# Loads of q and k by tile pairs, another pairing of heads, a shorter distance table, and a new order of all units

## The chip, the cores and the metric

The kernel runs on one core of a Trainium2 chip. The metric is the device time of one execution in microseconds, the median of several runs. Five engines of the core work side by side, each on its own queue of instructions in order: TensorE (PE in the profile, with its weight loads as PEld), VectorE (DVE), ScalarE (ACT), GpSimd (POOL), and SyncE (SP), which here only issues DMA transfers. They wait for one another by semaphores.

## What is computed

A causal attention with a local window and a few global keys, followed by a feed-forward layer that takes the maximum of three products:

```python
# q, k, v: (4 batches, 8 heads, 768 positions, 64), fp32;  n_global = 8, n_local = 96
scores = q @ k^T / sqrt(64)
rel = pos[:, None] - pos[None, :]
is_global = pos[None, :] < 8
is_local = (rel >= 0) & (rel < 96)
dist = where(is_global & ~is_local, 96, abs(rel))
scores = scores - slope[h] * dist          # slope[h] = 2 ** -(h + 1)
a = softmax(where(is_global | is_local, scores, -1e9))
x = (a @ v) as (3072 tokens, 512)
h = max(x @ w1, x @ w2, x @ w3)            # 512 -> 768
out = h @ w_out                            # 768 -> 512, fp32
```

The matrix products run in bf16 with fp32 sums.

## The kernel before

**Tiles.** The 3072 tokens are 24 tiles of 128, six per batch. A query tile needs its own key tile, the tile before it and the eight global keys. The global keys need no step of their own: the first eight rows of the key tile before are overwritten by the global ones (put_kg for k, put_vg for v) once that tile has served as its own.

**Units.** The work is cut into units, and a string, SCHEDULE, names them one after another; the loop at the end of the kernel (lines 479 and 480) calls them in that order, and every engine gets its instructions in the order of the calls. Nothing reorders them. A unit is a letter with numbers; the last number often chooses the engine (0 ACT, 1 DVE, 2 POOL).

- `l`, `c`, `x` (load_part, cast_part, u_x): for tiles 0 to 11, load q or k of a group of tiles from memory (SP), cast to bf16, transpose on TensorE into PSUM and copy back ("evacuate") into qkT, which holds head dimension by position. `L`, `C`, `X` (load, cast, u_X) do this tile by tile for tiles 12 to 23; with how = 4 a DMA transpose takes the place of TensorE and the evacuation. `v` and `C..1` load and cast v.
- `K` and `B` (u_K, u_B): from the table rbase of distances make, per head, a mask exp(-slope x distance) on ACT, or a bias -slope x distance. rbase is the distance where a key is allowed and 60000 where not.
- `S` (u_S): the scores of four heads of a tile, 64-row products on TensorE, and their exp on ACT into P. With how = 1 two further products with the identity add the bias; otherwise `M` (u_M) multiplies P by the mask on DVE.
- `A` (u_A): P times v with a column of ones, on TensorE; on DVE the reciprocal of the sums and the product into xb. `T` (u_XT) transposes xb into xT, on TensorE or (how = 4) by DMA.
- `F` (u_F1): for a chunk of two or four tiles, one of six column blocks f and one of three weights j: four products into a PSUM tile of the pool psH, which has three buffers. j = 0 is copied out by ACT, j = 1 and 2 are merged by DVE's maximum into ht. `O` (u_F2) and, for the last chunk, `E` (u_E): six products per tile with w_out, copy, and the output DMA.
- `w`, `W`, `o`, `Q`: loads and bf16 casts of the weights. `D`: products with zeros, which nobody reads. `G`, `V`: put_kg and put_vg.

**Ahead of the units** (lines 443 to 474) stand the first two loads, the table rbase, the identity for the transposes, and fills.

**Layout of q and k in tiles 0 to 11.** GROUPS cuts them into groups of 2, 2, 2, 4 and 2 tiles. A partition holds sz consecutive positions of every head of the part, so that a row of 64 x sz floats is contiguous in memory: 512 bytes for two tiles, 1 KB for four. A transpose takes a pair of neighbouring heads (2j, 2j + 1) of one of the sz positions; the evacuation puts the positions back in order. A score product of one head uses 64 of 128 rows, and two heads that lie in the two halves run side by side.

Of the kernel before, what the change touches and what calls it, by code (L numbers as in the profile page):

```python
# [12 lines left out]
FP32 = mybir.dt.float32  # L13
# [24 lines left out]
    O0.1.1 S9.1.0 S9.0.0 V7.1 M8.0 T6.0 x4.0.3 F1.2.2 M8.1 O0.2.1 M9.0 M9.1 C8.1.0 F2.5.0 F2.0.0
    G9.2 S10.0.0 S10.1.0 G10.2 F1.3.2 C9.1.2 F2.0.1 F2.0.2 A8.0 X12.0 F2.2.0 C13.0.3 V8.2 A9.1 X13.4
    T8.4 T9.4 F2.4.0 F2.5.1 C14.0.1 X14.4 v15 F2.4.1 S11.0.0 S11.1.0 O1.1.0 M11.0 M10.1 M10.0 F2.2.1  # L40
    S12.0.0 S12.1.0 F2.2.2 M11.1 F2.5.2 V9.2 C10.1.2 A10.0 V10.1 C11.1.2 L15 O1.0.0 F2.1.0 F2.4.2
    C13.1.2 A11.0 T10.0 F2.1.1 F2.3.0 S13.1.0 G12.0 S13.0.0 L18 T11.1 M12.1 F2.3.1 F2.3.2 M12.0
    G13.2 C15.1.2 L16 v14 C14.1.2 F3.5.0 F3.4.0 F3.4.1 F2.1.2 C12.1.0 M13.1 S14.0.0 M14.0 C15.0.0
    X15.4 S14.1.0 F3.5.1 M13.0 F3.1.0 A12.0 M14.1 F3.4.2 F3.2.0 F3.0.0 A13.0 V13.0 F3.1.1 C16.0.0
    G14.0 F3.2.1 F3.2.2 L19 F3.3.0 C18.0.0 X16.0 L17 F3.1.2 S15.1.0 S15.0.0 C19.0.1 T12.4 G15.0
    F3.3.1 F3.0.1 F3.0.2 X18.4 T13.4 C17.0.0 A14.1 F3.3.2 V14.1 F3.5.2 M15.0 X19.4 S16.0.0 L20 T14.4
    S16.1.0 M16.1 v18 C18.1.2 v17 v16 O2.0.0 X17.4 O3.2.0 S18.0.0 v19 S18.1.0 G16.0 O3.3.0 M15.1
    A15.0 V15.0 O3.1.0 C20.0.1 M18.1 X20.4 T15.0 M18.0 O3.0.0 F4.3.0 A18.0 M16.0 F4.2.0 F4.0.0
    S19.1.0 M19.1 C16.1.0 S19.0.0 L21 F4.0.1 F4.3.1 L22 A16.1 C19.1.0 L23 T16.4 F4.3.2 F4.2.1 G18.0
    V16.0 M19.0 F4.2.2 T18.4 S17.0.0 S17.1.0 F4.1.0 F4.5.0 F4.5.1 G19.2 M17.1 F4.1.1 A19.1 F4.1.2  # L50
    M17.0 F4.4.0 C17.1.2 F4.4.1 C21.0.3 F4.4.2 S20.0.0 S20.1.0 C22.0.1 F4.0.2 T19.4 F4.5.2 v20 X21.4
    A17.0 T17.4 O4.0.0 C23.0.0 X22.4 v21 O4.3.1 v22 V19.1 G20.0 O4.2.1 v23 O4.1.1 S21.0.0 S21.1.0
    F5.2.0 F5.1.0 M20.0 M21.0 M20.1 F5.1.1 C20.1.2 F5.5.0 F5.1.2 A20.1 M21.1 G21.2 F5.0.0 F5.2.1
    S22.0.0 V20.0 S22.1.0 G22.2 F5.5.1 F5.5.2 F5.0.1 F5.4.0 M22.0 C21.1.0 X23.4 S23.1.0 M23.1
    S23.0.0 F5.4.1 F5.4.2 A21.1 T21.4 V21.2 C22.1.2 M23.0 T20.4 O2.1.0 M22.1 F5.3.0 F5.3.1 C23.1.0
    F5.0.2 A22.0 T22.4 F5.2.2 F5.3.2 V22.2 A23.0 T23.4 O5.3.1 O5.0.1 O5.2.1 O5.1.1 F6.3.0 F6.1.0
    F6.1.1 F6.0.0 F6.4.0 F6.0.1 F6.4.1 F6.4.2 F6.5.0 F6.5.1 F6.1.2 F6.2.0 F6.2.1 F6.0.2 F6.2.2
    F6.3.1 F6.3.2 F6.5.2 E D2.8 D0.3
# [4 lines left out]
def kernel(  # L63
# [29 lines left out]
    GROUPS = [[0, 2], [2, 2], [4, 2], [6, 4], [10, 2]]  # L93
# [27 lines left out]
    identf = persist.tile([128, 128], FP32, name="identf")  # L121
# [24 lines left out]
    def part(n, s):  # L146

        T0, sz = GROUPS[n]
        jn = {2: 4, 4: 2, 6: 1}[sz]
        a, x = divmod(s, 4 // jn)  # L150
        return divmod(T0, NT) + (sz, a, x * jn, jn)

    def load_part(n, s):

        bb, t0, sz, a, j0, jn = part(n, s)
        r = raw_pool.tile([128, 2 * DM], FP32, name="rawp", tag="raw")
        r = r[:, 0:sz * jn * 128].rearrange("i (h x) -> i h x", h=2 * jn)
        raw["p", n, s] = r
        src = (q, k)[a][bb, 2 * j0:2 * (j0 + jn), t0 * 128:(t0 + sz) * 128, :]
        nc.sync.dma_start(out=r, in_=src.rearrange("h (i e) d -> i h (e d)", e=sz))  # L160
# [19 lines left out]
    def cast_part(n, s, how):  # L180
        bb, t0, sz, a, j0, jn = part(n, s)
        qk = cast_pool.tile([128, 2 * DM], BF16, name="qkp", tag="qkb")
        qk = qk[:, 0:sz * jn * 128].rearrange("i (e h d) -> i e h d", e=sz, d=D)
        qb["p", n, s] = qk
        copies[how](qk, raw["p", n, s].rearrange("i h (e d) -> i e h d", e=sz))  # L185

    def cast(T, what, how):
        b, t = divmod(T, NT)
        if what == 1:
            va[T] = va_first[b % 2] if t == 0 else va_ring[T % NVA]  # L190
            copies[how](heads(va[T])[:, :, 0:D], rawv[T])  # L191
# [3 lines left out]
        flat = raw[T].rearrange("p a h d -> p a (h d)")  # L195
        if how == 3:
            nc.vector.tensor_copy(qk[:, 0], flat[:, 0])
            nc.gpsimd.tensor_copy(qk[:, 1], flat[:, 1])
        else:
            copies[how](qk, flat)  # L200
# [27 lines left out]
    def u_x(n, s, how):  # L228
        bb, t0, sz, a, j0, jn = part(n, s)
        dst = batch_T(bb)[:, a, j0:j0 + jn, t0 * 128:(t0 + sz) * 128].rearrange("c j (i e) -> c j i e", e=sz)  # L230
        if how >= 4 and jn > 1:
            m = jn // 2
            halves = [(0, m, psT, "tp", nc.scalar.copy), (m, jn, psH, "h", nc.vector.tensor_copy)]
        else:
            pool, tag = (psH, "h") if how in (2, 3) else (psT, "tp")
            halves = [(0, jn, pool, tag, copies[how % 2])]
        tps = [pool.tile([128, sz, hi - lo, 128], BF16, name="tpp", tag=tag) for lo, hi, pool, tag, copy in halves]
        for (lo, hi, pool, tag, copy), tp in zip(halves, tps):
            for e in range(sz):
                for j in range(lo, hi):  # L240
# [273 lines left out]
```

## Time and profile before

| | |
|---|---|
| median of 3 runs (lowest to highest) | 178.89 us (178.78 to 180.11) |
| the profiled execution's own time | 179.17 us |
| its span | 177.4 us |
| TensorE clock granted, mean | 0.99 |
| PE busy | 170.6 us, 96% |
| DVE busy | 126.5 us, 71% |
| ACT busy | 109.7 us, 62% |
| POOL busy | 19.9 us, 11% |
| DMA packets, bytes | 85,730, 36.04 MB |

The page and the answers of the trace belong to one execution. The span begins with the first instruction that the profile shows and ends with the last; some 1.8 us of the execution lie outside it. Busy times are shares of the span, and an engine may be busy with work that nobody waits for. A busy share above 1 for DMA means that packets overlap on the 16 DMA engines. In the chain that ended last each step is followed back to what released it. A group of instructions is told by its line, engine, operation and tiles (out<-in).

### The profile page before, as it was taken

What the parts mean: (1) busy time and instruction counts of PE and PEld (TensorE: products, weight loads), DVE (VectorE), ACT (ScalarE), POOL (GpSimd) and SP (SyncE); (2) the same over time, 40 slices, a digit from 0 to 9 for tenths busy, and PEclk for the clock granted to TensorE, in tenths of its full rate; (3) what the DMA queues carried; (4) which work ended last, traced back from release to release, by engine and by line L of the source; (5) the groups of instructions that cost most, each with busy time, mean ns of one, the idle gap of its engine ahead of it and who ended that gap; (6) DMA issues with size and microseconds to landing.
All of it is one profiled execution on the core that took longest, in us unless ns stands there. A gap on an engine that the chain in (4) does not pass through costs nothing.

```text
span 177.4 us, 3967 instructions
## 1 busy us (share of the span) xinstructions
PE 170.6 (96%) x1550; PEld 95.7 (54%) x1550; DVE 126.5 (71%) x248; ACT 109.7 (62%) x166; POOL 19.9 (11%) x46
## 2 busy tenths in 40 slices
PE   7586899999999999999999999999999999999997
PEld 2344645458766786855554555455454555444444
DVE  4678969889697999769677557597667597435710
ACT  4979998758797967677595667615456630132022
POOL 4022300100130171010100011101000020000000
PEclk9879999999999999999999999999999999999999
DMA  5999999999999999899999999997796015600006
GB/s 146 291 234 271 344 343 381 321 356 325 289 211 221 241 301 147 214 242 204 213 175 186 208 245 248 231 164 148 176 300 91 0 33 134 218 32 0 4 21 215
DMA packets 85730, 36.04 MB, mean 203 GB/s; under 512 B 68304, under 2 KB 80464, under 8 KB 85712
## 3 DMA queue, kind: packets, MB, share of 16 engines
q1 hardware_dynamic: 85568, 35.73, 86.4%
q8 instruction: 12, 0.20, 0.5%
q10 hardware_dynamic: 144, 0.07, 0.1%
q14 instruction: 6, 0.05, 0.1%
HBM read 25.17 MB, written 6.29 MB: 177 GB/s over the span
## 4 chain that ended last, share of the span: by engine, by line
PE 90%; DMA 3%; issue 2%; ACT 2%; DVE 2%; SPq 0%; POOL 0%
PE h L363 54%; PE po L378 18%; PE sp L285 7%; DMA rawp<-in_k_dram 3%; PE op L324 3%; PE op L327 2%; PE tpp L241 2%; PE wp L440 2%; ACT P L290 1%; PE xtp L351 1%; PE sp L277 1%; DVE xb L334 1%; DVE qkp L185 1%; ACT qkT L245 1%; PE tp L263 1%
## 5 line engine op out<-in xcount | busy, mean ns | idle before, releaser
L363 PE MATMUL h<-xT,w 128*128 128x512 bf16 (+1 forms) x504 | 100.6, 349 | 0.0
L363 PEld LDWEIGHTS <-w 128*128 128x128 bf16 x504 | 46.9, 98 | 40.6 <-ACT w L429 0.2
L290 ACT ACTIVATE P<-sp 128x1024 bf16<-128x1024 f32 (+1 forms) x48 | 43.9, 956 | 12.3 <-PE sp L285 12.1
L368 ACT CAST h<-h 128x512 bf16<-128x512 f32 (+1 forms) x42 | 21.8, 529 | 30.8 <-PE h L363 29.0
L370 DVE TENSOR_TENSOR h<-h,h 128x512 bf16<-128x512 bf16 (+1 forms) x42 | 25.3, 608 | 14.9 <-PE h L363 10.4
L378 PE MATMUL po<-wo,ht 128*128 128x512 bf16 (+2 forms) x156 | 33.4, 363 | 0.0
L309 DVE TENSOR_TENSOR P<-P,wmask 128x1024 bf16<-128x1024 bf16 x38 | 25.4, 686 | 6.1 <-ACT P L290 5.8
L372 DVE TENSOR_TENSOR ht<-h,h 128x512 bf16<-128x512 bf16 (+1 forms) x42 | 25.5, 606 | 5.2 <-PE h L363 4.0
L378 PEld LDWEIGHTS <-ht 128*128 128x128 bf16 x156 | 14.2, 98 | 13.9
L334 DVE TENSOR_TENSOR xb<-op,rz 128x512 bf16<-128x512 f32 x24 | 16.6, 691 | 0.8
L384 ACT COPY ost<-po 128x512 f32<-128x512 f32 (+2 forms) x15 | 8.2, 555 | 14.5 <-PE po L378 14.4
L285 PE MATMUL sp<-qkT 64*128 64x128 bf16 x352 | 15.1, 221 | 0.9 <-ACT qkT L245 0.5
L285 PEld LDWEIGHTS <-qkT 64*128 64x128 bf16 x352 | 10.3, 96 | 9.8 <-issue 6.6
L324 PEld LDWEIGHTS <-P 128*128 128x128 bf16 x192 | 12.5, 97 | 3.6 <-DVE ht L372 0.5
L191 POOL CAST va<-rawv 128x512 bf16<-128x512 f32 x14 | 9.6, 692 | 41.0 <-DMA rawv<-in_v_dram 16.5
L384 DVE COPY ost<-po 128x512 f32<-128x512 f32 (+1 forms) x11 | 7.2, 653 | 9.2 <-PE po L378 9.1
L324 PE MATMUL op<-va,P 128*128 128x65 bf16 x160 | 12.5, 193 | 0.1
L327 PEld LDWEIGHTS <-P 128*128 128x128 bf16 x160 | 10.4, 97 | 1.5
L327 PE MATMUL op<-va,P 128*128 128x65 bf16 x128 | 9.9, 193 | 0.3 <-POOL va L223 0.3
L241 PE MATMUL tpp<-identb,qkp 128*128 128x128 bf16 x96 | 7.6, 227 | 2.2 <-DVE qkp L185 2.2
L245 ACT COPY qkT<-tpp 128x1024 bf16<-128x1024 bf16 (+1 forms) x8 | 7.3, 916 | 2.0 <-PE tpp L241 2.0
L241 PEld LDWEIGHTS <-qkp 128*128 128x128 bf16 x96 | 6.1, 101 | 3.8 <-DVE qkp L185 3.0
(65 smaller groups left out, 108.8 us busy)
## 6 DMA issues: line engine op xcount, KB each, us to landing
rawv<-in_v_dram SPq DMA_DIRECT2D x24, 256.0 KB, 5.3
out_dram<-ost SPq DMA_DIRECT2D x23, 256.0 KB, 3.7
rawp<-in_q_dram SPq DMA_DIRECT2D x6, 512.0 KB, 7.2
rawp<-in_k_dram SPq DMA_DIRECT2D x6, 512.0 KB, 7.2
wst<-in_moe_w_dram SPq DMA_DIRECT2D x3, 1024.0 KB, 10.8
raw<-in_q_dram SPq DMA_DIRECT2D x12, 256.0 KB, 5.3
raw<-in_k_dram SPq DMA_DIRECT2D x12, 256.0 KB, 5.1
wst<-in_moe_w_dram SPq DMA_DIRECT2D x3, 512.0 KB, 7.4
```

Source lines behind the costliest of these rows:

```text
L241: nc.tensor.transpose(tp[:, e, j - lo], qb["p", n, s][:, e, 2 * j:2 * j + 2].rearrange("i h d -> i (h d)"), identb)
L285: nc.tensor.matmul(sp[:, hh, j2, ds], qT(T - ds, 1)[hsl, jp], qT(T, 0)[hsl, jp], start=not how, stop=True, skip_group_check=True)
L290: nc.scalar.activation(P[:, :, 0:n], sp.rearrange("p a b d n -> p (a b) d n")[:, :, 0:n], AF.Exp, bias=0.0, scale=scale)
L309: nc.vector.tensor_mul(P, P, wmask[:, g, :, 0:2])
L324: nc.tensor.matmul(o, P[:, i, 0], heads(va[T])[:, h], start=True, stop=(t == 0), skip_group_check=True)
L327: nc.tensor.matmul(o, P[:, i, 1], heads(va[T - 1])[:, h], start=False, stop=True, skip_group_check=True)
L334: nc.vector.tensor_tensor(out=x.rearrange("p (g h) d -> p g h d", g=2), in0=o4[:, :, :, 0:64], in1=rz[:, :, :, None].to_broadcast([128, 2, ...
L363: nc.tensor.matmul(ps, w123[f // 2][:, dm, j, (f % 2) * 128:(f % 2) * 128 + 128], xT[c][:, dm], start=(dm == 0), stop=(dm == 3))
L368: nc.scalar.copy(h01, ps)
L370: nc.vector.tensor_max(h01s[c, f], h01s[c, f], ps)
L372: nc.vector.tensor_max(ht[c][:, f], h01s[c, f], ps)
L378: nc.tensor.matmul(po, ht[c][:, f, tt * 128:(tt + 1) * 128], wo[:, f, cols], start=(f == 0), stop=(f == NF - 1))
```

## The change

It has four parts.

1. **Loads by tile pairs.** GROUPS and part() are gone. Tiles 0 to 11 are six pairs; a load takes q (s = 0) or k (s = 1) of all eight heads of a pair in two DMAs of 256 KB, one for heads 0 to 3 and one for heads 4 to 7. A partition is one of four heads and one of 32 stretches of eight positions, so a row is 8 x 64 floats, 2 KB. Eight transposes follow per load, one per position within the stretch, and one evacuation, on ACT or DVE.
2. **Heads paired h and h + 4** in place of 2j and 2j + 1, in the transposes, scores, masks, biases and attention products; casts of tiles 12 to 23 put the heads in that order.
3. **The table of distances**: one iota in fp32 for both halves, one select for both and one for the first; the identity is made in bf16 directly, behind the table.
4. **A new SCHEDULE**: the same 487 units in another order and in part on other engines. Among them: the weight casts W0.0 and W0.2 and the casts of q of tiles 2 to 5 and k of tiles 4 and 5 go to POOL; q and k of tile 16 and x of tile 15 are transposed by DMA; the halves of tiles that get a bias (how = 1) are one of tile 0 and both of tile 3, where it was both of tile 0 and one each of tiles 1 and 3; of the dummies, 11 stand ahead of the first feed-forward product in both orders, and 9 in place of 11 at the end.

```diff
 SCHEDULE = """
...
+    K2 K5 K0 D4.2 K6 K3 B1.1 K1 D3.8 B4.1 K7 B3.0 B7.0 l1.1 c0.0.1 x0.0.0 l1.0 D1.1 B5.1 c0.1.1
+    x0.1.2 B0.1 B6.1 c1.1.1 B2.1 v0 x1.1.3 S0.1.0 S0.0.1 S1.1.0 C0.1.1 M0.1 c1.0.2 x1.0.3 S1.0.0 K4
+    M0.0 G0.2 G1.2 A0.1 l2.0 c2.0.2 M1.0 M1.1 S2.0.0 M2.0 S2.1.0 v1 C1.1.2 x2.0.3 M2.1 G2.2 S3.0.1
+    M3.0 S3.1.1 M3.1 l2.1 c2.1.2 T0.1 v2 G3.1 v3 C2.1.2 A1.0 V1.2 A2.1 V2.0 x2.1.0 C3.1.2 A3.0 w0.0
+    W0.0.2 T2.0 T1.0 T3.1 S4.0.0 S4.1.0 G4.2 w0.1 F0.1.0 w0.2 W0.2.2 F0.0.0 V3.0 S5.0.0 S5.1.0 w1.0
...
-    GROUPS = [[0, 2], [2, 2], [4, 2], [6, 4], [10, 2]]
+    ET = 8
...
     def load_part(n, s):
...
+        b, t0 = divmod(2 * n, NT)
+        r = raw_pool.tile([128, 2 * DM], FP32, name="rawp", tag="raw").rearrange("p (z x) -> p z x", z=2)
         raw["p", n, s] = r
+        src = (q, k)[s][b, :, t0 * 128:(t0 + 2) * 128, :]
+        for z in range(2):
+            nc.sync.dma_start(out=r[:, z], in_=src[4 * z:4 * z + 4].rearrange("h (i e) d -> i h (e d)", e=ET))
...
     def u_x(n, s, how):
...
+        b, t0 = divmod(2 * n, NT)
+        dst = batch_T(b)[:, s, :, t0 * 128:(t0 + 2) * 128].rearrange("c j (i e) -> c j i e", e=ET)
+        pool, tag = (psH, "h") if how in (2, 3) else (psT, "tp")
+        tp = pool.tile([128, ET, 128 // NP, NP], BF16, name="tpp", tag=tag)
+        for e in range(ET):
+            nc.tensor.transpose(tp[:, e].rearrange("c i j -> c (i j)"),
+                                qb["p", n, s][:, e].rearrange("p z d -> p (z d)"), identb)
+        copies[how % 2](dst, tp.rearrange("c e i j -> c j i e"))
...
     with tc.manual_schedule():
         load_part(0, 0)
...
+        load_part(0, 1)
+
+        BIGD = 60000.0
+        nc.gpsimd.iota(rbase[:, 0:2], base=0, pattern=[[128, 2], [1, 128]], channel_multiplier=-1,
+                       allow_small_or_imprecise_dtypes=True)
+        nc.vector.memset(tiny, 0.0)
+        nc.scalar.activation(tiny, tiny, AF.Exp, bias=0.0, scale=1.0)
...
+        nc.gpsimd.affine_select(rbase[:, 0:2], rbase[:, 0:2], base=(NL - 1),
+                                pattern=[[-128, 2], [-1, 128]], channel_multiplier=1,
+                                compare_op=ALU.is_ge, fill=BIGD)
```

More of the change, by code (lines that the diff above doesn't have):

```diff
@@ L228, in u_x @@
     def u_x(n, s, how):
[L229 to L240, printed above, removed]
-                    nc.tensor.transpose(tp[:, e, j - lo],
-                                        qb["p", n, s][:, e, 2 * j:2 * j + 2].rearrange("i h d -> i (h d)"), identb)
-        for (lo, hi, pool, tag, copy), tp in zip(halves, tps):
-            copy(dst[:, lo:hi], tp.rearrange("c e j i -> c j i e"))
+        b, t0 = divmod(2 * n, NT)
[6 more added lines that the diff above has]
+        copies[how % 2](dst, tp.rearrange("c e i j -> c j i e"))
     def u_X(T, how):
```

147 lines of the change are left out of this document (55 added, 92 removed).

## The prediction

> **What bounds the kernel now.** I read the page's busy times and slices first, then the same engines by stage, then the chain that ended last, and last the order of each engine's instructions in the first 24 us.
>
> ```profile
> PE 170.6 (96%) x1550; PEld 95.7 (54%) x1550; DVE 126.5 (71%) x248; ACT 109.7 (62%) x166; POOL 19.9 (11%) x46
> ...
> PE   7586899999999999999999999999999999999997
> ...
> DMA  5999999999999999899999999997796015600006
> ```
>
> TensorE is busy from the fifth slice to the end, and only the first slices have room. The table by stage (columns: stretch, its length, then busy us of PE, PEld, DVE, ACT, POOL, clock, DMA share, GB/s) puts numbers on that:
>
> ```profile
> 6.70:23.19 16.49, 12.99 (x194) 8.67 (x195) 13.07 (x25) 14.79 (x21) 3.71 (x8) 0.90 1.21 289
> 23.19:50.00 26.81, 26.81 (x249) 16.63 (x247) 22.52 (x42) 21.30 (x30) 1.80 (x3) 1.00 1.12 330
> ```
>
> From 23.19 us TensorE has no idle time. I counted its work there from steps in the chain: a 512-column product 0.216 us (16 in 3.45), a 256-column one 0.108, a transpose 0.056 (8 in 0.45), a score product 0.034 (16 in 0.55), an attention product 0.028. The products of the order behind 23.19 us come to 148.2 us, and the stretch to the end of the last output product (174.09) is 150.9: 2.7 us of small gaps. So the end is the first feed-forward product plus 148 us of work, plus gaps, plus a tail of 3.3 us. What can move much is the time of that first product. Before it ACT is busy 14.79 of 16.49 us and the DMA engines are full. The order of the last steps ahead of it, and of the end:
>
> ```profile
> 21.95 1.05 ACT L429 CAST w<-wst 128x1024 bf16<-128x1024 f32 x1
> ...
> 23.06 3.63 PE L363 MATMUL h<-xT,w 128*128 128x512 bf16 x16
> ```
> ```profile
> 174.09 2.38 PE wp L440 x11
> ```
>
> ACT casts the first weights at 21.95, after 18 us of its own queue, and the first product follows at 23.06.
>
> **The distance table.** Before: two iotas, two DVE casts, three selects and the identity ahead of them on POOL, then three DVE steps; ACT's first mask starts at 3.76. After: one iota and one select of 256 columns, one select of 128, the DVE steps, then the identity. No row has the wide forms: they lie between the narrow row (iota 0.24, select 0.29) and twice it; I take twice. From POOL's start at 0.73: 0.1 gap + 0.48 + 0.59 + 0.29 + the gaps of 0.06 + DVE 0.5 = about 2.85, so 0.9 us earlier (1.4 by the low ends). The identity comes at about 2.8, and its first user, a transpose, not before 5.5.
>
> **ACT's queue up to the first product.** Before, in order: 8 masks 3.9, 1 bias 0.5, evacuations of transposes 4.2, two exps of 0.6 and six of about 0.95, a global-row copy 0.4, two xT copies 1.15, the weight cast 1.05 = 18.1; from 3.76 that is 21.9, and it ended at 23.0, so 1.1 us was waiting. After: 8 masks 3.7, 2 biases 0.95, three evacuations 3.05, the same exps 6.9, copy 0.4, xT copies 1.15 = 16.2; the weight cast went to POOL. From 2.85, with the same 1.1 of waiting: 20.15. The evacuations read PSUM in another order of columns; no row shows it. Nearest are the present ones, 1.025 us on ACT and 1.217 on DVE for 1024 elements; the half-size rows (0.586, 0.684) times two say that order costs nothing. I take 0, with 0 to 0.5 us for the three on ACT.
>
> **The loads.** The six first q and k loads (3.1 MB) went in 512-byte rows, v in 256-byte rows, the first weights in 1-KB rows, the other weights in 2-KB rows:
>
> ```profile
> 3.00:4.50 1.50, 1.50 (x7) 0.52 (x5) 1.26 (x6) 0.74 (x2) 0.09 (x1) 1.00 1.14 337
> 8.00:10.00 2.00, 2.00 (x13) 0.74 (x11) 1.29 (x2) 1.74 (x4) 0.52 (x1) 0.50 1.23 281
> 10.00:12.00 2.00, 1.72 (x26) 1.32 (x26) 1.03 (x2) 1.17 (x2) 0.21 (x1) 0.80 1.35 219
> 20.00:22.00 2.00, 1.58 (x29) 1.23 (x29) 1.97 (x5) 1.66 (x5) 0.00 (x0) 1.00 1.10 348
> 28.00:30.00 2.00, 2.00 (x17) 1.00 (x16) 1.77 (x5) 1.97 (x4) 0.00 (x0) 1.00 1.05 387
> ```
>
> The reader sees 281 to 337 GB/s for 512-byte rows, 219 for 256, 348 for 1 KB, 387 for 2 KB. At 288 the 3.0 MB behind the ramp take 10.3 us. At 360, between the last two rows, 8.3: 2.0 us earlier for all that stands behind them on SP, the first weights too. The ends are 0.3 (337 against 348) and 2.6 (387). SP issues 12 instructions more; an issue into a free queue takes 0.45 us for what moves in 0.7, so SP doesn't bind. The Trainium skill ("DMA: Bandwidth & Descriptors", section "Why small descriptors are slow (HBM only)") gives three cycles of overhead per packet of 32-byte beats: 512 bytes would then run at 16/19 and 2 KB at 64/67 of the peak, a gain of 13%. By that rule the loads would save 1.2 us and not 2.0; the row of 387 against 281 says 38%, which other traffic blurs.
>
> **POOL.** It takes three q/k casts and the first weight cast of 1024 elements ahead of the first product. No row has that size: 512 elements take 0.61 alone and two back to back 1.17, so 1.2; the high end is twice the worst row below, 2.26. Its chain: q of tiles 2 and 3 lands at about 9.2 (cast to 10.4), the kg copies, q of tiles 4 and 5 about 11.9 (to 13.1), v1 to 13.7, k to 15.7, v2, a V copy, v3 to 17.8, then the first weights, landed at about 18.5, cast to 19.8. On the other side, tile 3's attention follows v3 at 18.0, DVE's xb to 19.5 and xT to 20.2. All three chains end between 19.8 and 20.2; I add 0.3 for contention: **first product at 20.5 instead of 23.06, so 2.5 us earlier.**
>
> **TensorE's work behind it.** Transposes of tile 16's q and k (8) and of tile 15's x (4) move to DMA: 12 x 0.056 = 0.7 us less. The DMA transposes land in 4.0 and 2.8 us; ten 512-column products of 0.86 per group stand between the former and its user, 6.7 us of work between the latter and its own. On SP each waits for its source, and the loads and outputs behind it wait with it; those are due later still. Uncovered, either would cost its landing time once. Two bias products fewer (tile 0) lie in the start stretch, where TensorE waits anyway: 0. Pairing heads h with h+4 changes which rows a product reads, not its size or count: 0; the L casts then run in pieces of 64, like the q/k cast rows (0.686) against the flat ones (0.745): 0.
>
> **New gaps.** In the new order VectorE has about 51 us of work in the first 51 us of TensorE's, with a surplus of some 3 us between the eighth and the seventeenth; only three PSUM buffers lie between them. And ACT's q/k casts of tiles 6 to 9 meet loads that land at 34 to 40 us while TensorE is 2.5 us further on: the exps of tile 6 stand behind the last of these casts. Walking both queues gives 0.5 to 1 us lost; the DMA stream itself is only 2.0 us ahead. I take 0.6, from 0 to 2.5 (the whole lead).
>
> **The tail.** The closing group is the same, but 9 dummies in place of 11 follow it. The chain ends with the dummies at 176.5, and the last output issued at 174.4 lands 1.9 us later, at 176.3: so -0.15 (0 to -0.43).
>
> **Sum.** -2.5 - 0.7 + 0.6 - 0.15 = -2.75 on the span of 177.4 and on the profiled execution's 179.17, hence 176.4. That execution lies 0.3 above the median of 178.89; against the median I forecast **176.1**.
>
> **Rivals.** (a) *The loads don't get faster*, because the stream is bound by bytes or by v's small rows (for: 337 GB/s with 512-byte rows alone; against: 281 a little later). The first weights land 1.7 us later, at 20.2, and are cast by 21.5; the later casts on ACT give back more: -1.4 - 0.5 + 1 = about 178.0. (b) *The lead is eaten by the full stream or by VectorE*, at the high end of the new gaps, 2.5 in place of 0.6: 178.0. For: ACT's wait for the casts of tiles 6 to 9; against: before, TensorE met the same full stream at 40 us without idling. (c) *Slower: POOL and VectorE block each other.* The rows of POOL:
>
> ```profile
> 34.88 0.61 POOL L191 CAST va<-rawv 128x512 bf16<-128x512 f32 x1 [14.97 <-DMA rawv<-in_v_dram]
> ...
> 49.43 1.13 POOL L191 CAST va<-rawv 128x512 bf16<-128x512 f32 x1 [2.47 <-PE h L363]
> ...
> 57.52 0.21 POOL L218 COPY qkT<-kg 128x32 bf16<-128x32 bf16 x1 [6.35 <-PE sp L285]
> 61.52 0.95 POOL L218 COPY qkT<-kg 128x32 bf16<-128x32 bf16 x1 [3.79 <-PE sp L285]
> ```
>
> The long ones began while VectorE cast (49.40 to 50.08) or multiplied two SBUF tiles (61.12 to 62.39), and ended about their own length after it. POOL runs 11 instructions, 8.0 us alone, from 9.2 to the first product. At the worst block of 0.74 each that is 25.3, first product 25.6, and with -0.7 and +0.6 -0.15 the end is 181.2. It decides from about 0.53 each; over the 16 v casts the mean block was 0.08 (692 against 615). The Trainium skill states the lock outright ("SBUF — State Buffer", section "Who interferes with whom"): a VectorE instruction in a two-port mode, or with two SBUF inputs against a POOL read, holds the shared port for its whole length. The trace agrees (0.21 against 0.95). (d) *Row size*: the 2-KB rows might be cut up again; packets would then stay near 85,700 in place of falling to about 80,000, and the time is that of (a).
>
> **Chances.** Forecast with its spread (t0 20 to 21.5, gaps 0 to 1) 0.60; (a), (b) and (d) together 0.25; (c) or another chain of the start later than before 0.15. The range runs from 173.9 (first product at 20.0, loads at their best, and a third of the 2.7 us of gaps gone too: -3.1 - 0.7 - 1.0 - 0.2) to 180.2, which leaves out the worst of (c). The likeliest case alone spans 174.8 to 177.1. One per cent, 1.8 us, is about what can be told from no change: faster 0.61, same 0.24, slower 0.15.
>
> **What would show it.** ACT's first mask at 2.8 to 2.9; k of tiles 0 and 1 landing at 6.3 (6.7 now); more than 340 GB/s from 4 to 8 us; the first weight cast on POOL from 18.5 to 19.8; the first product at 20.5; TensorE idle of about 0.6 us behind it; about 80,000 packets; casts of 1024 on POOL near 1.2. It is wrong if those casts take over 1.8, if the first weights land behind 20, or if TensorE shows gaps of more than 2 us between 30 and 60 us.

## The result, and the profile after

| | before | after |
|---|---|---|
| median of 14 runs each, side by side (lowest to highest) | 178.86 us (178.63 to 180.11) | 180.66 us (179.62 to 182.62) |
| ratio of the times, 95% interval | | 1.008 (1.0061 to 1.0098) |
| the profiled execution's own time, its span | 179.17, 177.4 us | 181.14, 179.4 us |
| first feed-forward product starts | 23.06 us | 25.38 us |
| from there to the start of the closing dummies | 151.03 us | 150.36 us |
| from there to the end of the span | 3.31 us | 3.66 us |

The changed kernel is 0.8% slower; 176.1 was forecast, and 180.66 lies above the range too. Ratios here and below leave out the runs that took over 1.5% more than their kernel's fastest (182.62 of the changed kernel, four of the twelve of e8_two_queues at 181.1 to 181.6, two of the six of e15_queues_kg_dummies at 180.6 and 180.7, and the longest one of e2, e5 and e16), while medians and ranges hold every run. The last three rows add up to the whole difference of the two profiled spans: +2.32 - 0.67 + 0.35 = 2.0 us. So the loss is in the start, ahead of the first feed-forward product, where the gain was forecast.

The page of the changed kernel (busy time by engine, TensorE's busy tenths, its granted clock, and the packets):

```profile
PE 169.0 (94%) x1513; PEld 95.6 (53%) x1534; DVE 127.4 (71%) x245; ACT 104.2 (58%) x158; POOL 24.8 (14%) x49
...
PE   7677589999999999999999999999999999999996
...
PEclk9969999999999999999999999999999999999999
...
DMA packets 80355, 36.44 MB, mean 203 GB/s; under 512 B 70096, under 2 KB 72016, under 8 KB 80336
```

ACT lost 5 us of work, POOL gained 5, and the packets fell from 85,730 to 80,355, all as the change says. TensorE's low digits now reach into the sixth slice, and the clock has a 6 in the third. The table by stage of the changed kernel shows why (columns as in the prediction: stretch, its length, busy us of PE, PEld, DVE, ACT, POOL, clock, DMA share, GB/s):

```profile
4.00:6.00 2.00, 2.00 (x10) 0.94 (x9) 0.96 (x2) 2.00 (x6) 0.00 (x0) 1.00 0.89 290
6.00:8.00 2.00, 0.95 (x6) 0.36 (x4) 0.72 (x2) 1.55 (x3) 0.00 (x0) 1.00 0.97 264
8.00:10.00 2.00, 0.62 (x8) 0.45 (x8) 1.23 (x4) 1.01 (x1) 0.00 (x0) 1.00 1.01 290
10.00:12.00 2.00, 1.97 (x24) 1.17 (x26) 1.46 (x3) 0.61 (x2) 1.19 (x2) 0.61 1.13 333
12.00:14.00 2.00, 2.00 (x30) 1.41 (x26) 1.30 (x4) 1.57 (x3) 0.19 (x2) 0.54 1.17 299
...
20.00:22.00 2.00, 1.06 (x23) 0.88 (x22) 1.97 (x4) 1.11 (x2) 1.69 (x3) 1.00 1.09 358
```

The same stretches of the kernel before:

```profile
4.00:6.00 2.00, 0.88 (x4) 0.20 (x2) 2.00 (x8) 2.00 (x6) 0.00 (x0) 1.00 1.21 302
6.00:8.00 2.00, 1.13 (x13) 0.96 (x14) 0.97 (x3) 1.63 (x3) 0.00 (x0) 0.85 1.21 290
```

From 4 to 10 us the changed kernel's loads run at 264 to 290 GB/s, where more than 340 were forecast for 4 to 8 us. The DMA share is 0.89 to 1.01, where before it was 1.21 to 1.23: the DMA engines aren't full. From 6 to 10 us every compute engine is idle for a good part, TensorE for 2.43 of 4 us, and TensorE comes out of that at about half clock. At 20 to 22 us VectorE is busy throughout, and ACT, which the prediction took for the bound of the start, is not. The chain that ended last, in order of time, tells the same (start, duration, what):

```profile
4.00 5.19 DMA rawp<-in_k_dram
...
9.28 0.71 DVE qkp L176
...
10.03 0.71 PE tpp L226 x8
...
12.38 0.98 PE tpp L226 x8
...
13.38 1.23 DVE qkT L228
...
14.75 0.69 DVE xb L313
15.44 2.71 DVE P L290 x3
18.16 1.14 DVE qkT L228
19.29 0.60 DVE P L290
...
20.23 1.50 DVE qkT L210
...
23.63 0.70 DVE xb L313
...
25.38 0.38 PE h L342
...
175.74 1.94 PE wp L419 x9
```

The first half is a load: k of tiles 2 and 3, behind which the new order puts the scores of tile 0. The second half is VectorE, without a gap from 13.38 to 24.33 us. Two rows in it are much too long, and the timeline of VectorE and POOL shows beside what they ran (start, duration, engine, line):

```profile
16.12 1.50 POOL L176 CAST qkp<-rawp 128x1024 bf16<-128x1024 f32 x1
16.64 1.52 DVE L290 TENSOR_TENSOR P<-P,wmask 128x1024 bf16<-128x1024 bf16 x1
17.56 1.07 POOL L182 CAST va<-rawv 128x512 bf16<-128x512 f32 x1
...
20.10 0.61 POOL L182 CAST va<-rawv 128x512 bf16<-128x512 f32 x1
20.15 1.58 DVE L210 COPY qkT<-kg 128x32 bf16<-128x32 bf16 x1
...
20.66 1.03 POOL L408 CAST w<-wst 128x1024 bf16<-128x1024 f32 x1
```

The multiply by a mask took 1.52 us, up to 0.54 after the end of the q/k cast on POOL; another of the same kernel took 0.68 in all. While that multiply ran, the next cast on POOL waited in its turn (1.07 us, and 0.61 for the same cast at 20.10). The copy of eight global key rows took 1.58 us: it began 0.05 after a cast on POOL had begun, and ended with the cast behind it. The same copy before:

```profile
15.22 0.17 DVE L218 COPY qkT<-kg 128x32 bf16<-128x32 bf16 x1
```

### The profile page after: what moved, and what is told of

Its sections match the earlier page's. It is cut to its first block, busy times and chain, and to the rows that moved or that the text cites. A ratio compares the mean times of both kernels' runs of the same rounds, so it can differ in the third digit from the quotient of the medians.

```text
span 179.4 us, 3940 instructions
## 1 busy us (share of the span) xinstructions
PE 169.0 (94%) x1513; PEld 95.6 (53%) x1534; DVE 127.4 (71%) x245; ACT 104.2 (58%) x158; POOL 24.8 (14%) x49
## 2 busy tenths in 40 slices
DMA packets 80355, 36.44 MB, mean 203 GB/s; under 512 B 70096, under 2 KB 72016, under 8 KB 80336
## 4 chain that ended last, share of the span: by engine, by line
PE 85%; DVE 7%; DMA 3%; SPq 2%; issue 1%; ACT 1%; ACTq 0%; DVEq 0%
PE h L342 52%; PE po L357 17%; PE sp L268 6%; DMA rawp<-in_k_dram 3%; PE op L303 3%; PE tpp L226 2%; PE op L306 2%; DVE P L290 2%; SPq L152 2%; DVE xb L313 2%; DVE qkT L228 1%; PE wp L419 1%; PE xtp L330 1%; DVE qkT L210 1%; ACT P L273 1%
## 5 line engine op out<-in xcount | busy, mean ns | idle before, releaser
L342 PE MATMUL h<-xT,w 128*128 128x512 bf16 (+1 forms) x490 | 99.4, 348 | 0.8
L290 DVE TENSOR_TENSOR P<-P,wmask 128x1024 bf16<-128x1024 bf16 x38 | 26.9, 731 | 3.4 <-ACT P L273 3.3
L363 ACT COPY ost<-po 128x512 f32<-128x512 f32 (+2 forms) x16 | 8.8, 554 | 23.3 <-PE po L357 23.2
L306 PEld LDWEIGHTS <-P 128*128 128x128 bf16 x160 | 10.5, 97 | 1.6
L226 PE MATMUL tpp<-identb,qkp 128*128 128x128 bf16 x96 | 8.3, 237 | 2.5 <-DVE qkp L176 2.5
L182 POOL CAST va<-rawv 128x512 bf16<-128x512 f32 x11 | 8.0, 725 | 19.1 <-PE h L342 11.5
L363 DVE COPY ost<-po 128x512 f32<-128x512 f32 (+1 forms) x10 | 6.4, 644 | 5.1 <-PE po L357 4.8
L312 DVE RECIPROCAL rz<-op 128x8 f32<-128x8 f32 x24 | 4.9, 202 | 7.3 <-PE op L306 6.3
L226 PEld LDWEIGHTS <-qkp 128*128 128x128 bf16 x96 | 6.7, 105 | 4.7 <-DVE qkp L176 3.8
```

What stands on the lines that cost most here:

```text
L226: nc.tensor.transpose(tp[:, e].rearrange("c i j -> c (i j)"), qb["p", n, s][:, e].rearrange("p z d -> p (z d)"), identb)
L290: nc.vector.tensor_mul(P, P, wmask[:, g, :, 0:2])
L306: nc.tensor.matmul(o, P[:, i, 1], heads(va[T - 1])[:, h], start=False, stop=True, skip_group_check=True)
L342: nc.tensor.matmul(ps, w123[f // 2][:, dm, j, (f % 2) * 128:(f % 2) * 128 + 128], xT[c][:, dm], start=(dm == 0), stop=(dm == 3))
```

## The experiments

All twelve stand in one table. "First exp" is ACT's, of tile 0; "DVE" is the start of VectorE's evacuation of q of tiles 2 and 3, from which its unbroken chain runs in the new order; "copy" is VectorE's copy of the global keys; "dense" is the time from the first feed-forward product to the closing dummies. The last six columns are of the profiled execution, whose own time stands in "profiled" (us). Where that is far from the median, as in e2, e5, e10, e12, e13 and e15, differences read from the trace are larger or smaller than those of the medians.

| run | median (lowest to highest) | ratio to before (95%) | profiled | first exp | DVE | copy | first product | dense |
|---|---|---|---|---|---|---|---|---|
| before | 178.86 | 1 | 179.17 | 9.32 | | | 23.06 | 151.03 |
| after | 180.66 | 1.008 (1.0061 to 1.0098) | 181.14 | 11.12 | 13.38 | 1.58 | 25.38 | 150.36 |
| e1_table | 179.34 (178.74 to 179.88) | 0.998 (0.996 to 1.000) | 179.74 | 9.43 | | | 23.61 | 151.08 |
| e2_old_order | 182.56 (181.24 to 184.00) | 1.015 (1.011 to 1.020) | 184.00 | 10.66 | | | 27.02 | 151.88 |
| e3_kg_act | 180.56 (179.16 to 181.42) | 1.005 (1.002 to 1.008) | 180.57 | 11.20 | 13.46 | none | 24.00 | 151.16 |
| e4_no_pool_casts | 182.32 (181.52 to 183.31) | 1.017 (1.013 to 1.021) | 182.62 | 11.23 | 14.53 | 0.17 | 26.86 | 150.07 |
| e5_s0_first | 182.04 (180.88 to 183.91) | 1.013 (1.009 to 1.018) | 183.91 | 10.01 | 14.10 | 0.16 | 26.92 | 151.78 |
| e8_two_queues | 178.52 (177.48 to 181.62) | 0.994 (0.991 to 0.996) | 178.86 | 9.72 | 11.35 | 0.60 | 22.31 | 151.34 |
| e10_table_two_queues | 181.06 (179.66 to 181.48) | 1.007 (1.004 to 1.010) | 179.95 | 10.04 | | | 23.79 | 151.09 |
| e12_whole_evac | 181.55 (180.66 to 183.00) | 1.013 (1.009 to 1.018) | 183.00 | 9.89 | | | 26.79 | 150.81 |
| e13_dummies | 179.68 (178.87 to 180.79) | 1.001 (0.997 to 1.005) | 178.87 | 10.87 | 12.51 | 0.59 | 23.47 | 150.18 |
| e14_queues_kg | 178.15 (177.45 to 179.02) | 0.992 (0.988 to 0.996) | 178.76 | 10.76 | 12.40 | none | 22.94 | 150.58 |
| e15_queues_kg_dummies | 179.10 (177.46 to 180.68) | 0.994 (0.989 to 0.998) | 180.64 | 11.45 | 13.09 | none | 23.62 | 151.79 |
| e16_no_pool_dummies | 184.11 (182.43 to 185.68) | 1.023 (1.018 to 1.028) | 183.51 | 11.15 | 14.14 | 0.16 | 27.04 | 150.80 |

Ratios are against runs of before in the same sitting (medians 178.86 to 179.51).

**The table of distances alone**, in the kernel before:

```diff
-        nc.gpsimd.iota(rbase[:, 0, :].bitcast(mybir.dt.int32), base=0,
-                       pattern=[[1, 128]], channel_multiplier=-1,
+        nc.gpsimd.iota(rbase[:, 0:2], base=0, pattern=[[128, 2], [1, 128]], channel_multiplier=-1,
...
+        nc.gpsimd.affine_select(rbase[:, 0:2], rbase[:, 0:2], base=(NL - 1),
+                                pattern=[[-128, 2], [-1, 128]], channel_multiplier=1,
+                                compare_op=ALU.is_ge, fill=BIGD)
```

> The kernel before with the new distance table alone. ACT's first mask should start at 2.7 to 2.9 us in place of 3.76. If ACT's queue bounds the stretch ahead of the first feed-forward product, that product comes 0.7 to 0.9 us earlier (22.2) and the time is about 178.0. If the landing of the first loads bounds it, ACT only waits longer for them: first product at 22.9 to 23.1, time within 0.3 of 178.9.

ACT's first mask starts at 2.71 us instead of 3.76, yet its first exp is at 9.43 (9.32 before) and the first product at 23.61. VectorE's timeline in this run shows what holds both:

```profile
5.12 0.70 DVE L184 CAST qkp<-rawp 128x1024 bf16<-128x1024 f32 x1 [0.77 <-DMA rawp<-in_q_dram]
...
6.93 0.69 DVE L184 CAST qkp<-rawp 128x1024 bf16<-128x1024 f32 x1 [0.84 <-DMA rawp<-in_k_dram]
```

VectorE stands idle ahead of both casts, until the load lands. The microsecond that ACT's queue got ahead became waiting: the loads bind the start already in the kernel before. The interval of the time reaches 1.

**The new loads and table under the old order.** The schedule of before, with its loads of tiles 6 to 11 renamed for pairs, and its two evacuations that were shared by ACT and VectorE made whole:

```diff
-    K2 K5 K0 D4.2 K6 K3 B1.1 K1 D3.8 B4.1 K7 B3.0 B7.0 l1.1 c0.0.1 x0.0.0 l1.0 D1.1 B5.1 c0.1.1
...
+    K6 K5 D1.2 D4.8 B2.1 B4.1 B7.1 B5.1 l1.0 l1.1 K4 B6.1 v0 B1.0 B3.1 c0.0.1 K1 K3 x0.0.2 K7 B0.1
+    c0.1.1 x0.1.3 G0.2 c1.0.1 c1.1.1 K0 S0.0.1 S1.1.1 M1.1 S1.0.0 G1.2 x1.0.3 S0.1.1 x1.1.0 K2 M0.0
```

> The new loads, head pairs and table under the order of the kernel before (its parts of tiles 6 to 9 renamed to pairs, its two split evacuations made whole, one on ACT and one on DVE). If the new order is what costs the time and the new loads are good, the first product comes at 21.5 to 22.5 and the time is 177 to 178. If the new loads land later and hurt any order, the first product comes behind 23.3 and the time is 179.3 to 181.

1.015, and the first k cast waits 1.81 us and starts at 7.41 (6.74 before): the loads are late in either order, so the new order isn't what makes them so. But what the layout costs can't be read from this run, because a part of its edit does as much alone:

**Two whole evacuations**, in the kernel before with the new table:

```diff
-    c0.1.1 x0.1.4 G0.2 c1.0.1 c1.1.1 K0 S0.0.1 S1.1.1 M1.1 S1.0.0 G1.2 x1.0.3 S0.1.1 x1.1.0 K2 M0.0
+    c0.1.1 x0.1.3 G0.2 c1.0.1 c1.1.1 K0 S0.0.1 S1.1.1 M1.1 S1.0.0 G1.2 x1.0.3 S0.1.1 x1.1.0 K2 M0.0
...
-    w0.1 x2.1.4 T3.1 W0.0.0 S4.0.0 W0.1.1 S4.1.0 w0.2 D3.1 F0.0.0 G4.1 M4.1 M4.0 F0.1.0 F0.1.1
+    w0.1 x2.1.2 T3.1 W0.0.0 S4.0.0 W0.1.1 S4.1.0 w0.2 D3.1 F0.0.0 G4.1 M4.1 M4.0 F0.1.0 F0.1.1
```

> The kernel before with the new table, its two evacuations that were split between ACT and DVE made whole (k of tiles 0 and 1 on DVE, k of tiles 4 and 5 on ACT), as the new layout forces them. If the loss of the split explains the new layout under the old order (first product at 27.0 against 23.6), the first exp starts at about 10.0 in place of 9.4, the first product at 24.5 or later, and the ratio to before is 1.004 or more. If the loads are at fault, the first product stays below 24.0 and the ratio is 0.998 to 1.002.

1.013 (its profiled execution is the longest of its runs). The first exp is 0.46 us later than with the table alone, the first product 3.18. Its table by stage:

```profile
10.00:12.00 2.00, 2.00 (x21) 1.06 (x20) 0.69 (x1) 1.09 (x2) 0.28 (x2) 0.50 1.35 219
...
18.00:20.00 2.00, 1.78 (x16) 0.76 (x16) 2.00 (x4) 1.22 (x3) 0.00 (x0) 0.50 1.13 344
```

In these rows TensorE is busy, but its clock is 0.50 all the way from 10 to 22 us, where e1_table has 0.50 and 0.70 from 8 to 12 and 1.00 after. That the clock makes the 3 us is argued from these rows and not shown: no run of this order has more dummies.

**The copy of the global keys from VectorE to ACT**, in the changed kernel:

```diff
-    M3.0 S3.1.1 M3.1 l2.1 c2.1.2 T0.1 v2 G3.1 v3 C2.1.2 A1.0 V1.2 A2.1 V2.0 x2.1.0 C3.1.2 A3.0 w0.0
+    M3.0 S3.1.1 M3.1 l2.1 c2.1.2 T0.1 v2 G3.0 v3 C2.1.2 A1.0 V1.2 A2.1 V2.0 x2.1.0 C3.1.2 A3.0 w0.0
```

> The changed kernel with one small copy, the global keys into tile 3, on ACT in place of DVE. On DVE it took 1.58 us against 0.17 elsewhere, while POOL cast. If POOL and DVE blocking each other sets the end of the start stretch, DVE reaches tile 1's reciprocal 1.3 us earlier, the first product comes at about 24.1 in place of 25.4, and the time is 179.4 against 180.7. If tile 1's attention waits for something else anyway (v casts on POOL, exps), the gain is at most 0.4: 180.3 or more.

The first product starts 1.38 us earlier: the copy, and with it VectorE, was on the path. Of that, the dense part gave back 0.80 (151.16 for 150.36). It is one wait, far behind the start: TensorE stands until the DMA transpose of x of tile 17, issued at 121.76, has landed (a line of the chain, and one of TensorE's waits: us, times, longest):

```profile
121.76 3.27 DMA xT<-xb
...
PE h L342 <- DMA xT<-xb: 0.8, 1, 0.8
```

The changed kernel has no such wait. The interval of the ratio, 1.002 to 1.008, overlaps that of the changed kernel. So the block is shown in the trace, and in the time it is worth less than these runs tell.

**Tile 0's scores ahead of the transposes of k of tiles 2 and 3**, in the changed kernel:

```diff
-    x0.1.2 B0.1 B6.1 c1.1.1 B2.1 v0 x1.1.3 S0.1.0 S0.0.1 S1.1.0 C0.1.1 M0.1 c1.0.2 x1.0.3 S1.0.0 K4
+    x0.1.2 B0.1 B6.1 c1.1.1 B2.1 v0 S0.1.0 S0.0.1 S1.1.0 x1.1.3 C0.1.1 M0.1 c1.0.2 x1.0.3 S1.0.0 K4
```

> The changed kernel with the transposes of k of tiles 2 and 3 moved behind the first three score units, so that tile 0's scores don't stand behind the landing of that load on TensorE. The first exp should start at 9.8 to 10 us in place of 11.1. If the late start of the scores sets the first product, it comes about 1 us earlier (24.4) and the time is about 179.7. If POOL's casts and their blocking of DVE set it, it moves by less than 0.4: 180.3 or more.

The first exp comes 1.11 us earlier, at 10.01, and the first product 1.54 later; the ratio is 1.013. VectorE's chain now starts at 14.10, and one of its multiplies meets a short copy and two casts in a row on POOL (19.83 to 21.77):

```profile
19.86 2.45 DVE L290 TENSOR_TENSOR P<-P,wmask 128x1024 bf16<-128x1024 bf16 x1
```

2.45 us instead of 0.68: it is through 0.54 after the last of them has ended, as above, so most of it is waiting. The ratio is some 0.5% above that of the changed kernel with overlapping intervals, so what holds is that an earlier first exp gains nothing here; the trace puts that on VectorE's chain.

**No q/k or first-weight casts on POOL**, in the changed kernel (c1.0, c2.0 and c2.1 to VectorE, W0.0 and W0.2 to ACT):

```diff
-    W0.0.2 T2.0 T1.0 T3.1 S4.0.0 S4.1.0 G4.2 w0.1 F0.1.0 w0.2 W0.2.2 F0.0.0 V3.0 S5.0.0 S5.1.0 w1.0
+    W0.0.0 T2.0 T1.0 T3.1 S4.0.0 S4.1.0 G4.2 w0.1 F0.1.0 w0.2 W0.2.0 F0.0.0 V3.0 S5.0.0 S5.1.0 w1.0
```

> The changed kernel with the five long casts of the start taken off POOL: q of tiles 2 to 5 and k of tiles 4 and 5 to DVE, two first weight casts to ACT. If POOL's casts and DVE blocking each other cost the start its lead, DVE loses about 2.9 us of blocked time (multiplications of 1.52 and one copy of 1.58 back to 0.68 and 0.17) and gains 2.1 us of casts; first product at about 24.0 in place of 25.4, ratio to before 1.000 to 1.003. If DVE's own work then binds, the first product stays at 25.0 to 25.8 and the ratio at 1.006 or more.

1.017: with less work on POOL in the way VectorE's copy takes 0.17, its three multiplies 2.31 instead of 2.77, and yet the first product starts at 26.86. TensorE's clock is 0.50 from 8 to 20 us in this run. To tell the clock from the casts, the same kernel with 14 more dummies:

```diff
-    K2 K5 K0 D4.2 K6 K3 B1.1 K1 D3.8 B4.1 K7 B3.0 B7.0 l1.1 c0.0.1 x0.0.0 l1.0 D1.1 B5.1 c0.1.1
+    K2 K5 K0 D4.2 K6 K3 B1.1 K1 D3.8 B4.1 K7 B3.0 B7.0 l1.1 c0.0.1 x0.0.0 l1.0 D1.5 B5.1 c0.1.1
+    x0.1.2 D5.6 B0.1 B6.1 c1.1.1 B2.1 v0 x1.1.3 S0.1.0 S0.0.1 S1.1.0 C0.1.1 M0.1 c1.0.1 x1.0.3
+    S1.0.0 D5.4 K4 M0.0 G0.2 G1.2 A0.1 l2.0 c2.0.1 M1.0 M1.1 S2.0.0 M2.0 S2.1.0 v1 C1.1.2 x2.0.3
```

> The changed kernel without long casts on POOL in the start, with the dummies at the waits for the first k loads and 4 more ahead of q of tiles 2 and 3. Without dummies the clock lay at 0.50 from 8 to 22 us and the first product came at 26.9. If the half clock hid what the freed DVE gained, the first product now comes at 24.0 to 24.8 and the ratio is 1.002 to 1.005. If DVE's added casts are the bound, the clock is up and the first product still comes behind 25.4, ratio 1.008 or more.

The clock is now 1.00 up to 22 us, and the first product is no earlier, 27.04 (23.47 in e13_dummies below, which has the casts on POOL and ten of these dummies). The casts that VectorE took back stand in its chain (timeline of VectorE):

```profile
16.54 0.68 DVE L176 CAST qkp<-rawp 128x1024 bf16<-128x1024 f32 x1
...
21.10 1.45 DVE L176 CAST qkp<-rawp 128x1024 bf16<-128x1024 f32 x1
```

The second took 1.45 us for 0.68: a copy and a cast of v on POOL (20.57 to 22.00) still hold it up. So the casts were better placed on POOL. What costs is where they meet VectorE's instructions.

**Ten more dummies alone**, in the changed kernel:

```diff
-    K2 K5 K0 D4.2 K6 K3 B1.1 K1 D3.8 B4.1 K7 B3.0 B7.0 l1.1 c0.0.1 x0.0.0 l1.0 D1.1 B5.1 c0.1.1
+    K2 K5 K0 D4.2 K6 K3 B1.1 K1 D3.8 B4.1 K7 B3.0 B7.0 l1.1 c0.0.1 x0.0.0 l1.0 D1.5 B5.1 c0.1.1
+    x0.1.2 D5.6 B0.1 B6.1 c1.1.1 B2.1 v0 x1.1.3 S0.1.0 S0.0.1 S1.1.0 C0.1.1 M0.1 c1.0.2 x1.0.3
```

> The changed kernel with 10 more products of zeros that fill TensorE's waits for the first k loads (5 in place of 1 ahead of the first k transposes, 6 behind them). In the changed kernel the granted clock was 0.61 and 0.54 from 10 to 14 us. If the clock that falls while TensorE waits costs the start part of its lead, it reads 1.00 there, the scores of tiles 0 and 1 run at full speed, the first product comes at about 24.4 in place of 25.4 and the ratio to before is 1.002 to 1.004. If the landing of the loads and the blocking of DVE by POOL set the first product, the clock is up and the first product still comes within 0.4 of 25.4, ratio 1.006 or more.

1.001, with an interval that lies below that of the changed kernel: 0.7% or 1.2 us for products that nobody reads (the profiled execution is the shortest of its runs). Its table by stage, to be held against 0.62 us of work at 8 to 10 and a clock of 0.61 and 0.54 behind it:

```profile
8.00:10.00 2.00, 1.75 (x14) 1.04 (x15) 1.69 (x5) 1.01 (x1) 0.00 (x0) 1.00 1.05 326
10.00:12.00 2.00, 1.85 (x30) 1.20 (x29) 1.35 (x2) 1.13 (x3) 1.19 (x2) 1.00 1.10 340
12.00:14.00 2.00, 1.27 (x27) 1.04 (x26) 1.97 (x5) 2.00 (x4) 1.17 (x3) 1.00 1.15 304
```

The first product is 1.91 us earlier in the trace, which isn't all the clock: VectorE's chain starts 0.87 earlier (0.45 of that is k of tiles 2 and 3, cast at 8.83 instead of 9.28), and the copy takes 0.59 instead of 1.58, because by then the weight cast on POOL was still waiting for its load.

**The first k load issued by ACT instead of SP**, in the changed kernel; nothing else is changed:

```diff
-            nc.sync.dma_start(out=r[:, z], in_=src[4 * z:4 * z + 4].rearrange("h (i e) d -> i h (e d)", e=ET))
+            eng = nc.scalar if (n, s) == (0, 1) else nc.sync
+            eng.dma_start(out=r[:, z], in_=src[4 * z:4 * z + 4].rearrange("h (i e) d -> i h (e d)", e=ET))
```

> The changed kernel with both halves of the first k load issued by ACT at its start, beside SP's q load. If SP's 0.6 us per issue sets when the first loads land, k of tiles 0 and 1 lands at about 6.2 in place of 7.25, k of tiles 2 and 3 at 8.2 in place of 9.25, the first exp starts at about 10.1 in place of 11.1, and the first product moves up by 0.5 to 1.0. If the DMA engines deliver what they deliver (270 to 290 GB/s in this stretch), k lands at 6.9 or later and the time moves by less than 0.3.

0.994: 1.4% less than the changed kernel. By the means of all its runs it is 0.999 (179.25 us for 179.36), and the changed kernel by the same means 1.009. So it is below the changed kernel either way; that it beats the kernel before is not shown. Its table by stage, against 290 and 264 GB/s in the changed kernel:

```profile
4.00:6.00 2.00, 1.67 (x4) 0.30 (x2) 0.67 (x2) 2.00 (x6) 0.00 (x0) 1.00 1.06 390
6.00:8.00 2.00, 1.48 (x17) 0.98 (x17) 1.91 (x6) 2.00 (x5) 0.00 (x0) 1.00 1.02 385
```

Over 4 to 8 us together, the seven profiles of this layout with all loads on SP have 260 to 288 GB/s, the three with this edit 368 to 396. One queue comes near that only in single stretches and later: up to 336 GB/s from 6 to 8 us (e4_no_pool_casts) and up to 346 from 8 to 10 (e5_s0_first). VectorE's casts of the first two k loads, which now wait for nothing (7.28 and 9.28 in the changed kernel, with waits of 1.70 and 0.77):

```profile
6.31 0.69 DVE L177 CAST qkp<-rawp 128x1024 bf16<-128x1024 f32 x1
...
7.61 0.69 DVE L177 CAST qkp<-rawp 128x1024 bf16<-128x1024 f32 x1
```

ACT's table load and masks start 1.0 later for it (first mask 3.72), and q lands 0.7 later (cast at 5.33). The loads no longer bind this start; ACT's queue does, which runs from the first mask to its second evacuation almost without a pause (timeline of ACT), and the scores of tile 0 follow that evacuation at 9.39:

```profile
3.72 2.98 ACT L284 ACTIVATE wmask<-rbase 128x384 bf16<-128x384 f32 x7
...
7.44 1.89 ACT L229 COPY qkT<-tpp 128x1024 bf16<-128x1024 bf16 x2
```

VectorE's chain starts 2.03 us earlier, the copy takes 0.98 less, and the first product is 3.07 earlier (0.5 to 1.0 was expected). TensorE's clock stays at 1.00 without a dummy more.

**The same in the kernel before**, with the new table and its own 512-byte rows:

```diff
-        nc.sync.dma_start(out=r, in_=src.rearrange("h (i e) d -> i h (e d)", e=sz))
+        (nc.scalar if (n, s) == (0, 1) else nc.sync).dma_start(out=r, in_=src.rearrange("h (i e) d -> i h (e d)", e=sz))
```

> The kernel before with the new table, and its first k load issued by ACT at its start. ACT has 1.5 us of waiting there since the table is ready. If issue time counts, k lands at about 6.3 in place of 6.9, the first exp at 8.9 in place of 9.4, and the ratio to before is about 0.995, faster than both kernels. If the engines' rate counts, nothing moves: ratio 0.998 to 1.000.

1.007: it loses (five runs took 179.7 to 180.2 us, the profiled one among them, and six 181.1 to 181.5). Here the engines are full with one queue already (first row e10_table_two_queues; e1_table had 1.20 and 306):

```profile
4.00:6.00 2.00, 1.28 (x4) 0.30 (x2) 0.35 (x2) 1.30 (x4) 0.00 (x0) 1.00 1.19 309
```

A second queue adds no bytes; q, which had the stream to itself, shares it and is cast at 6.24 instead of 5.12, and k at 7.17 instead of 6.93.

**Both edits, and dummies as well**: the k load on ACT with the copy on ACT, and then five more dummies:

```diff
-    x0.1.2 B0.1 B6.1 c1.1.1 B2.1 v0 x1.1.3 S0.1.0 S0.0.1 S1.1.0 C0.1.1 M0.1 c1.0.2 x1.0.3 S1.0.0 K4
+    x0.1.2 D5.4 B0.1 B6.1 c1.1.1 B2.1 v0 x1.1.3 S0.1.0 S0.0.1 S1.1.0 C0.1.1 M0.1 c1.0.2 x1.0.3
```

> The changed kernel with the first k load issued by ACT and the copy of the global keys into tile 3 on ACT. With the two queues alone that copy still took 0.60 on DVE, and the first product came at 22.3. If the start sets the time, the first product comes at 21.7 to 22.0 and the ratio to before is 0.988 to 0.993, below both kernels. If the lead is given back to the loads of the weights and of tiles 6 to 9, the ratio is that of the two queues alone, 0.994, or above.

> The one with two queues and the copy on ACT, with 5 more products of zeros at the waits for the first k loads. With two queues alone 4 of 12 runs were 3 us longer, with a mean clock of 0.98 to 0.99 against 1.00. If those are runs in which the clock fell in the start stretch, dummies keep it up, and no run lies more than 1 us above the median, ratio 0.988 to 0.994. If not, the long runs stay.

(The fifth dummy is D1.2 for D1.1.) The pair of edits gives 0.992, the fastest of all here, though it can't be told from the k load alone (0.994). The dummies add nothing once the clock holds without them. They were also to keep every run within 1 us of the median; two of six are at 180.6 and 180.7, with a mean clock of 1.00, so the clock isn't what makes these long. The trace is of one of them, 1.88 us longer than that of e14_queues_kg: 0.68 in the start, where 2.0 us of dummies stand in the chain (0.43 in e14), and 1.21 in the dense part, where TensorE waits 1.39 at 103 us for a copy on VectorE. In the profiled executions of both q and k land later than in e8_two_queues (q cast at 6.15 and 6.09 for 5.33), with the same loads: a single trace's landing is good to some 0.8 us only, and the three agree on the rate (390, 403 and 375 GB/s at 4 to 6 us) better than on the times.

One sum holds in six runs of the new order with its casts on POOL. From the start of VectorE's chain to the first product it is 12.00, 10.54, 10.96, 10.96, 10.54 and 10.53 us in after, e3, e13, e8, e14 and e15; less the copy it is 10.4 to 10.5 in each, with some 0.8 of one multiply's waiting in it. So the first product is the start of that chain, plus 10.4, plus the copy with what it is made to wait. In e5_s0_first it is 12.82, 1.77 of them the wait of its other multiply: which instruction meets POOL changes with the start.

Not tried: a single transfer of 512 KB in 2-KB rows, which would tell the size of the transfers from the number of queues.

## Why the prediction was wrong, step by step

- **What bounds it**, the first product plus some 151 us, held: dense is 150.1 to 151.9 us in all fourteen profiles, while the first product moves from 22.3 to 27.0.
- **Distance table**: right. The first mask is at 2.71 (2.85 forecast); the wide iota took 0.35 and the wide select 0.41, between the ends that were set.
- **ACT's queue, "with the same 1.1 of waiting"**: this step failed. Its work is as listed; the evacuations in the new column order cost 1.01 on ACT and 1.22 on VectorE, so the order of columns costs nothing, as taken. But the waiting was not a constant. It is what is left when the work comes before the loads, and e1_table shows it: one microsecond less work ahead, no earlier exp. In the changed kernel ACT waits 1.12, 1.41, 1.41 and 1.58 us in single pieces up to the first product, and isn't the bound any more. It is again in the first 9 us of e8_two_queues, where the loads come in time.
- **The loads, "2.0 us earlier"**: this step failed, and most of the miss hangs on it. The rate for 2-KB rows was read from a stretch (28 to 30 us) where SP's queue had 1-MB transfers in it. In the start the same rows came from 256-KB transfers on one queue, at 260 to 288 GB/s over 4 to 8 us and with the engines not full. The other half of the step, that SP doesn't bind because an issue takes 0.45 us, was off too: each of the small ones took SP 0.58 to 0.65. That alone isn't the limit, since by 6 us SP had issued eight of them, 2.1 MB, and some 1.1 MB had moved. With a second queue the rate is 368 to 396, more than the 360 that was forecast. So the larger row was worth what was said, and one queue of 256-KB transfers didn't bring it over these 4 us; why, with a megabyte issued ahead, no run here shows. The Trainium skill ("DMA: Bandwidth & Descriptors", section "Issuing engines are not separate DMA queues") says that issuing from several engines saves only the sequencer's time, usually little. That time is 1.3 us here (SP is through with q of tiles 2 and 3 at 4.60 instead of 5.90), but the rate rises as well, so in this start the measurement goes beyond the page.
- What came of it: k of tiles 0 and 1 was cast at 7.28 (landing at 6.3 was forecast, 6.74 before), q of tiles 2 and 3 on POOL at 10.80 (9.2). By 20 us the stream was ahead by 0.35 MB, some 1.0 us instead of 2.0.
- **POOL's chain**: a cast of 1024 elements takes 1.04 us alone (1.2 taken), and e16_no_pool_dummies shows POOL to be the better place for them. The chain's eleven instructions are 7.0 us alone (8.0 taken), and yet it ends at 21.7 instead of 19.8: its first load came 1.6 late, behind that POOL waited 1.81 and 0.30 for scores on TensorE, and blocking took 1.4. The first weight cast ran from 20.66 to 21.69.
- **"All three chains end between 19.8 and 20.2; I add 0.3 for contention"**: this step failed in its second half. VectorE's chain was followed by its ends (xb at 19.5) and not by its sum. From the evacuation at 13.38 on it has 8.7 us of work of its own and 2.25 of blocking: 1.41 in the copy and 0.84 in one multiply. Blocking was the mechanism of rival (c), but the payer is the other engine. POOL's own eleven instructions lost 1.4 us in all, 0.13 each, far below the 0.53 from which (c) was to decide; VectorE, which stands in the path, lost 2.25. So (c) came close with its 25.6 for the first product, and for another reason.
- **The clock** was not in the sum at all, though the profile of before had 0.50 at 8 to 10 us. Late loads leave TensorE idle, and it comes back at half speed: e13_dummies puts 0.7% on that, with the copy's better timing in it. How much is the clock's stays open: among the changed kernel's own runs the time doesn't follow the mean clock (180.3 to 180.9 us at 0.971, 179.8 to 181.2 at 0.99).
- **TensorE's work behind it**: Dense is 0.67 shorter, which agrees with the 12 transposes' 0.7. **New gaps** of 0.6 don't show in the changed kernel, nor by the start being earlier: dense is 150.18 in e13 and 150.58 in e14, 151.16 in e3 and 151.34 in e8. What the last two have more is the one wait of 0.8 and 1.2 us for the DMA transpose of x of tile 17, near 124 us, and not VectorE's surplus or ACT's late casts, so these runs don't bear rival (b) out.
- **The tail** came out 0.35 longer instead of 0.15 shorter. The last output is issued 0.38 us behind the last product (0.33 before) and lands as fast; the other 0.3 was not followed.
- **Packets**: 80,355 (80,000 forecast), which rules out rival (d). Rival (a) had the cause, loads that don't get faster, and put it at 178.0, since it let the start gain 1.4 us all the same.

In sum: -2.5 was forecast for the first product and +2.32 came. Loads on two queues take 3.07 of these 4.8 us back (e8_two_queues), of which 0.98 is the copy's blocking that went with it; the remaining 1.8 lies in ACT's queue ahead of VectorE's chain, in the rest of VectorE's blocking and in its queue, which was never walked through; these three weren't told apart. One sum of the chances is off too: by its own ends (first product 20 to 21.5, gaps 0 to 1) the likeliest case spans 175.0 to 177.5, not 174.8 to 177.1, which changes nothing here.

## What to carry to other kernels

Read the gain of a larger row from transfers of the same size, on the same queue and with the same backlog, and check the DMA share: where it is below that of a full stream (0.93 against 1.21 from 4 to 8 us here), try a second queue before a larger row. Work taken off an engine that waits for loads turns into waiting, and a pause of TensorE can cost again after it, in clock. Long casts on GpSimd are cheap until VectorE's copies and two-input operations meet them on the path, so walk VectorE's queue through as a sum and put its short copies elsewhere.

## What was not expected of the hardware

- A copy of 128 x 32 elements took 1.58 us (0.17 alone) and a multiply 2.45 (0.68 alone): each waited until two POOL casts in a row had ended, and was not let in between them. Another multiply (1.52) was let in between two casts, and the second cast waited instead; what decides that, no run here shows.
- In the changed kernel TensorE's granted clock fell to 0.54 to 0.61 for some 4 us once it had worked 1.57 of 4 us (6 to 10 us), and stayed at 1.00 where ten dummies made that 3.30. The Trainium skill ("TensorE: Matmul & The Clock Gate", "Part 1: The HAM clock gate") gives half speed as the state after an idle window; the traces agree in the level (0.50 from 11 to 13 us). In e4_no_pool_casts it stayed at 0.50 for 12 us with TensorE 1.04 to 2.00 of every 2 us busy.
- Two 256-KB loads on ACT's queue took the stretch from 4 to 8 us from at most 288 to at least 368 GB/s for 2-KB rows; for 512-byte rows it was 295 to 299, with one queue (three kernels) and with two (one).
